# Thresholded attention and two feed-forward layers on one core: Mish as one ScalarE function, one power-of-two set per pair, other warm-up, other plan

## The chip, the core and the metric

The kernel runs on one core of one Trainium2 chip. The core's engines are TensorE (PE in the profile; PEld is its weight load), VectorE (DVE), ScalarE (ACT), GpSimd (POOL) and SyncE (SP), which only issues transfers. The metric is the device time of one execution in microseconds. Of the kernel before there are three such times, 1044.63, 1046.04 and 1046.65, median 1046.04, and one profiled execution.

## What is computed

Attention over 4 batches, 8 heads, 576 rows, 64 columns, in which a score counts only if it lies within tau of its row's maximum; then two feed-forward layers over the 2304 rows of 512, with 2048 hidden columns. The weights come as 64-bit floats.

```python
scores = scale * np.matmul(q, k.transpose(0, 1, 3, 2))
thresh = np.max(scores, axis=-1, keepdims=True) - tau
scores = np.where(scores >= thresh, scores, -1000000000.0)
attn = softmax(scores)                 # written out in the reference
x = (attn @ v), heads side by side     # 2304 x 512
h = x @ w_in;  x = (np.maximum(h, 0.0) ** 2) @ w_out          # first layer
h = x @ w2_in
sp = np.where(h > 20.0, h, np.log1p(np.exp(np.minimum(h, 20.0))))
out = (h * np.tanh(sp)) @ w2_out                              # second layer
```

## The kernel before

The kernel is written as a list of operations, and a planner in the kernel file puts them in order. Each operation (`op`) names the engines that may run it with a cost for each, the buffers that it reads (`r`), writes (`w`) or changes (`x`), and a due time. `Plan.order` builds a timetable by these costs, goes over it backwards to set the due times anew and forwards again (`fbi` times), and the program is issued in the order of the last timetable. So the table `PAR`, the numbers `BIAS` and the costs in the `op` calls set the order on every engine; each engine then runs its own queue strictly in that order and waits on semaphores.

Attention. Heads go in pairs, four pairs in each batch. A pair has four units of two heads by 128 rows and one tail unit of 64 rows of either head. `unit` issues the scores, a scan on DVE for the row maximum (`top`), the threshold (`most`: one addition), the exponential on ACT and the mask with the row sum on DVE (`mask`, both in `weigh`). A pair is of one of three kinds. "d" (direct): scores in float32, the weights of a head turned by five PE transposes (`values_direct`), values in float32 (`turned`), results turned back. "s" (split): q, k and v are scaled by powers of two (`pow2` finds them from the sums of squares, with one small PE product over the `ones` tile to add over the partitions, then four small DVE steps) and split into two float16 parts each (`split`); scores are three float16 products, the weights are split too (`high`, `low`), turned by a DMA transpose and multiplied by both parts of v. "h" (mixed): scores as in "d", values as in "s". Batch 0 is dddd, batch 1 is hhsh (`kb`), batches 2 and 3 are ssss.

Layers. Both layers work on blocks of 256 rows (nine). The numbers are held as a high and a low part, and each product is three products of parts (`passes`). Every piece of weights is converted once per layer from its 64-bit form (`weights`: `size`, `rest`, `clamp`, `shift`, `sign` or `factor` and `times`, then the high part `to_hi` and the remainder `to_lo`); layer 2's pieces take the places of layer 1's as these come free, while the last block of layer 1 still runs. `first` and `first_part` are layer 1: 24 matmuls of 256 columns into `h`, relu and square, rounding, remainder, 24 matmuls into `acc`; `x_first` brings a block of the attention's result from DRAM, turns it and makes its parts `xh` and `xo`. The nine blocks of layer 1 run between the units of attention. `second` is layer 2: two blocks at a time with 512 columns per matmul, one block alone at the end; between the two products stand exp, `cap`, log, `add`, sigmoid and `gate`, with a change of ACT's function table ahead of the exp and ahead of the sigmoid.

Start. `consts` makes `ident` and `ones` and loads tau; `warm` puts PE transposes of `ones` that nothing reads into the queue, six pairs of them at the plan's start, two and three behind the first two turnings of q and k.

Of the kernel before, what the change touches and what calls it, by code (L numbers as in the profile page):

```python
# [22 lines left out]
E20 = 485165195.40978996  # L23

# [6 lines left out]
    merge=3,  # L31
    warm=(6, 2, 3),
    won=("S", "S"),
    land=2.09,
    lag=0.886,
    turns=("h",),
    kv=(("nat0", "V1"), ("f1", "nat1"), ("KT1", "f0"), ("V0", "KT0")),
    cd=(-128.498, 12.059, -64.352),
    urg=-19.282,
    rawt=19.972,  # L40
    kinds="dddd",
    cgen=0.135,
    split=(),
    ex=dict(cw=1, cr=6, raw=13, pd=2, sc=3),
    exo=("cw", "sc", "pd", "cr", "raw"),
    blk=list((56.005, 116.765, 222.843, 298.566, 412.468, 531.531, 625.519, 840.505, 1014.576)),
    tb2=133.298,
    down2=-115.407,
    sp=(0, 3),
    off=(205.994, 56.765, 32.779, -218.536, 74.356, 29.099, -131.451, -101.025),  # L50
    ahead=(6.306, 90.66, 9.794, -93.49, 14.671, 183.136, 42.58, 390.333, 192.204, -47.067),
    start=-111.506,
    area=dict(sc=("x0", "x1"), hl=("x2",)),
    jobahead=19.363,
    fbi=7,
    stay=-17.176,
    kinds2="ssss",
    kb=("hhsh", "ssss", "ssss"),
# [23 lines left out]
class Plan:  # L82
# [6 lines left out]
    BIAS = {"V": 1.874, "A": -0.818, "P": 2.37, "S": 0.46}  # L89
# [3 lines left out]
    TICK, ENTRY = 3.4133, 1.275  # L93

# [12 lines left out]
    def op(self, opts, fn, r=(), w=(), x=(), due=0.0, load=None, tab=None, two=False, half=False):  # L107
# [93 lines left out]
    def forwards(self, succ):  # L201
# [7 lines left out]
        table, half = None, False  # L209
# [14 lines left out]
        while count < len(ops):  # L224
            best = None
            for e in engs:
# [41 lines left out]
                if e == "T" and ops[pick].half != half:  # L268
                    same = [n for _, n in now if ops[n].half == half and ops[n].due < ops[pick].due + PAR["stay"]]
                    if same:  # L270
                        pick = same[0]
# [28 lines left out]
            if e == "T":  # L300
                dur += 0.1 * (half and not o.half)
                half = o.half
# [18 lines left out]
def attention_moe_moe_kernel(ctx: ExitStack, tc: tile.TileContext, q, k, v, tau, w1i, w1o, w2i, w2o, out):  # L321
# [119 lines left out]
    K = plan.buf("const", lambda: None)  # L441

    def consts(e):
        make_identity(nc, ident)
        nc.gpsimd.memset(ones, 1.0)
# [14 lines left out]
    def weights(layer, kind, j, due, places, wplaces, merged=False):  # L460
# [17 lines left out]
        for half in range(1 if merged else 2):  # L478
# [27 lines left out]
            def upper(raw=raw):  # L506
                return raw()[:, :, 1]
# [8 lines left out]
            def size(e, w=w, upper=upper):  # L516
                if e == "A":
                    nc.scalar.activation(out=w(), in_=upper().bitcast(F32), func=AF.Abs, scale=W_SCALE)
# [41 lines left out]
            op(cost(0.09, A=0.56, P=0.71), size, r=[raw], w=[w], due=due - 4, two=2)  # L560
            op({**cost(0.11, A=0.56, P=0.71), **cost(V=0.34)}, rest, x=[raw], due=due - 3.5 + O_CV, two=2)
            op(cost(V=0.34, P=0.71), clamp, x=[w], due=due - 3 + O_CV, two=2)
            op(cost(0.06, V=0.6), shift, r=[raw], x=[w], due=due - 2 + O_CV, two=1)
# [933 lines left out]
```

## Time and profile before

| | |
|---|---|
| median of three runs | 1046.04 us |
| the profiled execution | 1046.22 us, its span 1044.4 us |
| PE busy | 1016.4 us (97%), 8582 matmuls |
| PEld busy | 885.0 us (85%) |
| ACT busy | 796.4 us (76%), 72 table loads in it: 92.4 us |
| DVE busy | 744.0 us (71%) |
| POOL busy | 51.7 us (5%) |

The page's second part cuts the span into 40 slices. By its busy digits DVE is at 9 or 8 up to about 494 us, PE at 9 from 130 us on, ACT at 7 to 9 nearly throughout. A busy share is an average over stages with different limits, and a busy PE can still be at half its clock: the granted clock of each stretch stands beside it. The first layer's first matmul comes at 131 us, the second layer's first at 641. Between the end of the last matmul and the end of the span lie the last evacuation and the last stores.

### The profile page before, as it was taken

The numbers are of one execution on the slowest core, as the hardware profiler recorded it, in microseconds if no ns is written. First come the engines' busy times: TensorE is split into PE (matmuls) and PEld (weight loads), VectorE is DVE, ScalarE is ACT, GpSimd is POOL, SyncE is SP. The second block draws the span as 40 slices with busy tenths as digits, with TensorE's granted clock in tenths as the row PEclk, the third lists the DMA queues.
The fourth block names the chain that finished last, engine by engine and source line by source line (L and its number), as shares of the span: only waits on it lengthen the run. The fifth ranks groups of instructions, "written<-read, shape, count | busy, mean of one in ns | idle before, by whom it ended". The sixth has DMA issues, their size and how long they took to land.

```text
span 1044.4 us, 22116 instructions
## 1 busy us (share of the span) xinstructions
PE 1016.4 (97%) x8582; PEld 885.0 (85%) x8582; DVE 744.0 (71%) x1693; ACT 796.4 (76%) x1277; POOL 51.7 (5%) x53
## 2 busy tenths in 40 slices
PE   6999799999999999999999999999999999999998
PEld 2666479888988898998999999978888888888897
DVE  3999999999888998998672138788754544544533
ACT  3789888886877877786794459999976877786765
POOL 0210132000010000000000000000000000000000
PEclk9999899999999999999999999999999999999999
DMA  8624467888977988887761013421100110010010
GB/s 259 176 68 146 143 141 168 154 164 150 178 156 158 164 181 159 178 170 138 189 199 66 26 66 101 142 88 53 48 34 1 41 41 1 21 41 1 1 42 20
DMA packets 238521, 111.48 MB, mean 107 GB/s; under 512 B 202320, under 2 KB 219216, under 8 KB 238416
## 3 DMA queue, kind: packets, MB, share of 16 engines
q1 hardware_dynamic: 238128, 109.55, 44.4%
q8 instruction: 67, 1.10, 0.4%
q10 hardware_dynamic: 288, 0.52, 0.1%
q14 instruction: 38, 0.31, 0.1%
HBM read 58.13 MB, written 14.16 MB: 69 GB/s over the span
## 4 chain that ended last, share of the span: by engine, by line
PE 80%; ACT 10%; DVE 5%; issue 3%; DMA 1%; SPq 0%; DVEq 0%; ACTq 0%
PE acc L428 25%; PE h L428 21%; PE s L428 20%; PE small L428 10%; ACT area L1266 2%; DVE e L900 1%; ACT L1262 1%; PE acc L750 1%; PE s L790 1%; ACT area L530 1%; PE s L1169 1%; ACT gh L576 1%; DVE area L866 1%; ACT area L554 1%; ACT e L889 1%
## 5 line engine op out<-in xcount | busy, mean ns | idle before, releaser
L428 PE MATMUL h<-xh,wi 128*128 128x256 f32 x1152 | 218.5, 282 | 0.4 <-ACT r L1214 0.4
L428 PE MATMUL acc<-gh,wo 128*128 128x256 f32 x1152 | 215.7, 280 | 0.0
L428 PEld LDWEIGHTS h<-xh,wi 128*128 128x128 f32 x1152 | 184.4, 193 | 10.3 <-issue 4.7
L428 PEld LDWEIGHTS acc<-gh,wo 128*128 128x128 f32 x1152 | 183.1, 192 | 5.5 <-issue 4.7
L428 PE MATMUL h<-xo,wi 128*128 128x256 f32 x576 | 159.0, 276 | 0.0
L428 PE MATMUL acc<-gl,wo 128*128 128x256 f32 x576 | 158.5, 275 | 0.0
L428 PEld LDWEIGHTS h<-xo,wi 128*128 128x128 f32 x576 | 111.1, 193 | 0.0
L428 PEld LDWEIGHTS acc<-gl,wo 128*128 128x128 f32 x576 | 110.6, 192 | 0.0
L428 PE MATMUL s<-KT,area 64*128 64x512 f16 (+7 forms) x820 | 95.6, 358 | 4.0 <-DVE xo L1186 2.3
L1262 ACT ACT_TABLE_LOAD x72 | 92.4, 1283 | 1.3
L587 DVE TENSOR_TENSOR gl<-r,gh 128x512 fp32r<-128x512 f32 x80 | 55.3, 691 | 51.5 <-ACT gh L576 49.8
L889 ACT ACTIVATE e<-area,m 128x576 f32<-128x576 f32 x93 | 70.6, 771 | 18.9 <-DVE area L866 8.6
L428 PE MATMUL acc<-wo,gh 128*128 128x512 f32 x240 | 79.8, 380 | 0.0
L900 DVE SCALAR_TENSOR_TENSOR e<-area,n,e 128x576 f32<-128x576 f32 x93 | 74.4, 814 | 6.0 <-ACT e L889 5.1
L576 ACT ACTIVATE gh<-r 128x512 fp32r<-128x512 f32 x90 | 56.5, 628 | 27.5 <-PE acc L428 24.3
L1214 ACT ACTIVATE r<-h 128x512 f32<-128x512 f32 x72 | 42.8, 595 | 39.8 <-PE h L428 34.4
L866 DVE TENSOR_SCALAR_CACHE_REDUCE area<-s,c 128x576 f32<-128x576 f32 x81 | 64.9, 814 | 5.3 <-PE s L428 4.5
L929 DVE TENSOR_TENSOR hl<-e,hl 128x512 f16<-128x512 f32 (+1 forms) x137 | 67.5, 499 | 1.4 <-ACT hl L924 1.1
L428 PE MATMUL small<-V,pt 128*128 128x64 f16 (+1 forms) x1680 | 65.5, 194 | 0.3 <-DMA pt<-hl 0.3
L1266 ACT ACTIVATE area<-area 128x512 f32<-128x512 f32 x108 | 63.7, 621 | 0.3
L924 ACT ACTIVATE hl<-e 128x576 f16<-128x576 f32 x77 | 52.0, 677 | 15.3 <-DVE e L900 12.0
L428 PEld LDWEIGHTS <-pt 128*128 128x128 f16 (+1 forms) x1680 | 54.9, 101 | 10.2 <-issue 7.5
(299 smaller groups left out, 2223.6 us busy)
## 6 DMA issues: line engine op xcount, KB each, us to landing
area<-in_moe_w_in_dram SPq DMA_DIRECT2D x13, 512.0 KB, 3.7
area<-in_moe_w_out_dram SPq DMA_DIRECT2D x12, 512.0 KB, 3.9
xx<-xdr SPq DMA_DIRECT2D x36, 128.0 KB, 2.6
x2dr<-stg SPq DMA_DIRECT2D x18, 256.0 KB, 2.3
xdr<-xx SPq DMA_DIRECT2D x32, 128.0 KB, 2.2
area<-in_moe_w_in_dram SPq DMA_DIRECT2D x4, 1024.0 KB, 5.5
wi<-in_moe_w_out_dram SPq DMA_DIRECT2D x3, 1024.0 KB, 5.1
f<-in_v_dram SPq DMA_DIRECT2D x12, 256.0 KB, 3.0
```

What stands on the lines that cost most here:

```text
L428: nc.tensor.matmul(o, l, r, start=start, stop=stop, skip_group_check=True)
L530: nc.scalar.activation(out=lower(), in_=lower().bitcast(U32), func=AF.Copy, scale=0.93 * 2.0 ** -29)
L576: nc.scalar.activation(out=o, in_=i, func=AF.Copy)
L587: VEC[e].tensor_tensor(out=part(lo), in0=src(), in1=f32(part(hi)), op=ALU.subtract)
L866: nc.vector.tensor_scalar(out=sc(), in0=s()[:, 0:576], scalar1=c()[:, 3:4], scalar2=None, op0=ALU.mult, op1=ALU.min, accum_out=m()[:, i:i ...
L889: lambda e: nc.scalar.activation(out=ex(), in_=sc(), func=AF.Exp, bias=m()[:, i:i + 1], scale=-1.0),
L900: nc.vector.scalar_tensor_tensor(out=ex(), in0=sc(), scalar=nt()[:, i:i + 1], in1=ex(), op0=ALU.is_le, op1=ALU.mult, accum_out=l()[:, 0, u ...
L924: nc.scalar.activation(out=hl()[:, 0:576], in_=ex(), func=AF.Copy)
L929: VEC[e].tensor_tensor(out=hl()[:, a:a + n], in0=ex()[:, z:z + n], in1=hl()[:, z:z + n], op=ALU.subtract)
L1214: nc.scalar.activation(out=halves(r()), in_=turned_out(ph()), func=AF.Relu)
L1262: nc.scalar.preload_act_table_set({"ln": "natural_log_exp_and_others", "sig": "sigmoid_and_others"}[table])
L1266: nc.scalar.activation(out=out, in_=in_, func=func, **kw)
```

## The change

It does the following.

- `second`: the six steps between layer 2's products become one ACT function, Mish, read from PSUM; its table is loaded once.
- `job`: k, q and v of a split pair share one call of `pow2` (three columns instead of two and one), so v is loaded and split in `job` too. `job_v` stays for mixed pairs.
- `warm`: single products of `ones` by `ones` into eight slices of `acc` in turn, which need only `ones`, instead of pairs of transposes into one slice; 1, 3 and 7 of them. `ones` is filled by an operation of its own, ahead of `ident`.
- The last block's sums: the two tiles of `acc` are buffers of their own, in the last step each tile's products are operations of their own, and the second tile is evacuated and stored in two halves.
- `unit`: the scores' matmuls go from 64 columns and then 512 to 512 and then 64; `most` may run on ACT.
- The plan: new numbers in `PAR`, `BIAS` and costs. By them batch 1 is dhss instead of hhsh, weights are no longer converted in double pieces (`merge` 8 instead of 3), `factor` and `times` are not used, and POOL gets nothing but constants.

```diff
-    merge=3,
-    warm=(6, 2, 3),
+    merge=8,
+    warm=(1, 3, 7),
...
-    sp=(0, 3),
+    sp=(0, 0),
...
-    kb=("hhsh", "ssss", "ssss"),
+    kb=("dhss", "ssss", "ssss"),
...
-    BIAS = {"V": 1.874, "A": -0.818, "P": 2.37, "S": 0.46}
+    BIAS = {"V": 1.26, "A": 0.34, "P": 3.463, "S": 0.46}
...
-    K = plan.buf("const", lambda: None)
+    K, K0 = plan.buf("const", lambda: None), plan.buf("ones", lambda: None)
+    op({"P": 0.5}, lambda e: nc.gpsimd.memset(ones, 1.0), w=[K0], due=-60.0)
...
+        rv = sbuf(place("f", "f0", "f1", "f2"), [128, 10, 64], F32)
...
-        isc = pow2("kq", [rk, rq], [kn, qn], due - 8)
+        isc = pow2("kqv", [rk, rq, rv], [kn, qn, V], due - 8)
...
-        job_v(p, due - O_JOB)
+        split(rv, 2, c, V, lambda: V()[:, :, 0:64], lambda: V()[:, :, 64:128], due - 5, 640)
...
+    def spin(i):
+        if not spun:
+            spun.append(psum.tile([128, 1024], F32, name="acc", tag="acc"))
+        z = 128 * (i % 8)
+        mm(spun[0][:, z:z + 128], ones, ones, True, True)
...
-                for c0, c1 in ((512, 576), (0, 512)):
+                for c0, c1 in ((0, 512), (512, 576)):
...
-        op({"V": 0.12}, most, r=[m, K], w=[nt], due=due + 1.3 - URG)
+        op({"V": 0.12, "A": 0.2}, most, r=[m, K], w=[nt], due=due + 1.3 - URG)
...
+        def mish(out, in_):
+            if not loaded:
+                nc.scalar.preload_act_table_set("mish")
+                loaded.append(1)
+            nc.scalar.activation(out=out, in_=in_, func=AF.Mish)
...
+                    op({"A": 0.48}, gate, r=[ph[z].buf], w=[gs[z]], due=d + 0.6, tab=("sig",))
+                    to_hi(gs[z], ghs[z], flat, d + 0.8)
+                    to_lo(gs[z], ghs[z], gls[z], flat, d + 0.9)
+                work = [(f, n, (0, 1)) for f in range(nf) for n in range(k)]
+                if end and st == 16 // nf - 1:
+                    work = [(f, 0, (t,)) for t in range(2) for f in range(nf)]
...
+                    for c0, c1 in ((0, 128), (128, 256)) if end and t else ((0, 256),):
```

The order on PE at the program's start, up to the second unit of scores, before (`ident,wo` are the turnings of q and k, `ident,ones` the warm-up, `KT,area` scores):

```order
L790 MATMUL s_102<-ident,wo_72 128x128 x4
L790 MATMUL s_102<-ident,wo_72 128x64
L790 MATMUL s_114<-ident,wo_72 128x128 x4
L790 MATMUL s_114<-ident,wo_72 128x64
L750 MATMUL acc<-ident,ones 128x128 x8
L428 MATMUL s_144<-KT,area 128x64
L428 MATMUL s_146<-KT,area 128x64
L428 MATMUL s_144<-KT,area 128x512
L428 MATMUL s_146<-KT,area 128x512
L750 MATMUL acc<-ident,ones 128x128 x14
L428 MATMUL s_199<-KT,area 128x64
```

And now, the same place:

```order
L435 MATMUL acc<-ones 128x128
L806 MATMUL s_114<-ident,wo_74 128x128 x4
L806 MATMUL s_114<-ident,wo_74 128x64
L806 MATMUL s_127<-ident,wo_74 128x128 x4
L806 MATMUL s_127<-ident,wo_74 128x64
L435 MATMUL acc<-ones 128x128 x4
L435 MATMUL s_150<-KT,area 128x512
L435 MATMUL s_152<-KT,area 128x512
L435 MATMUL s_150<-KT,area 128x64
L435 MATMUL s_152<-KT,area 128x64
L435 MATMUL acc<-ones 128x128 x6
L435 MATMUL s_184<-KT,area 128x512
```

Ahead of the first scores stand four products (and one at the very start) where eight transposes stood, and ahead of the second unit six where fourteen stood.

The order on DVE from its first weight conversion to the first scans of scores (`s_144`, `s_146` and `s_199` are read by the scans), before:

```order
L525 TENSOR_SCALAR stg<-stg 128x512
L542 SCALAR_TENSOR_TENSOR stg<-stg,area 128x512
L548 SCALAR_TENSOR_TENSOR stg<-area,stg 128x512
L587 TENSOR_TENSOR wi_109<-stg,wi_109 128x512
L525 TENSOR_SCALAR wo_138<-wo_138 128x512
L542 SCALAR_TENSOR_TENSOR wo_138<-wo_138,xh 128x512
L866 TENSOR_SCALAR wo_138,m_170<-s_144,cd 128x576
L866 TENSOR_SCALAR wi_188,m_170<-s_146,cd 128x576
L548 SCALAR_TENSOR_TENSOR wo_138<-xh,wo_138 128x512
L875 TENSOR_SCALAR n_207<-m_170,tt 128x2
```

And now (the scans read `s_150` and `s_152`):

```order
L555 SCALAR_TENSOR_TENSOR wo_92<-xh,wo_92 128x512
L532 TENSOR_SCALAR stg<-stg 128x512
L594 TENSOR_TENSOR wo_112<-wo_92,wo_112 128x512
L549 SCALAR_TENSOR_TENSOR stg<-stg,area 128x512
L555 SCALAR_TENSOR_TENSOR stg<-area,stg 128x512
L594 TENSOR_TENSOR wi_136<-stg,wi_136 128x512
L532 TENSOR_SCALAR stg<-stg 128x512
L549 SCALAR_TENSOR_TENSOR stg<-stg,area 128x512
L532 TENSOR_SCALAR stg<-stg 128x512
L555 SCALAR_TENSOR_TENSOR stg<-area,stg 128x512
L882 TENSOR_SCALAR wi_168,m_169<-s_150,cd 128x576
L882 TENSOR_SCALAR wo_176,m_169<-s_152,cd 128x576
```

Twelve conversion steps stand ahead of the first scan (the first two are above the piece shown) where six stood, and the threshold addition has left DVE.

The order on ACT in layer 2, one step of two blocks and the beginning of the next, before (`s_10712` is a product in PSUM, `r` and `stg` go into the rounding):

```order
L1262 ACT_TABLE_LOAD
L1266 ACTIVATE area<-s_10712 128x512 x2
L1266 ACTIVATE area<-area 128x512 x2
L1262 ACT_TABLE_LOAD
L1266 ACTIVATE area<-area 128x512 x2
L576 ACTIVATE pt_10855<-r 128x512
L576 ACTIVATE gh_10857<-stg 128x512
L1262 ACT_TABLE_LOAD
```

And now:

```order
L1282 ACTIVATE r<-s_10206 128x512
L1282 ACTIVATE stg<-s_10206 128x512
L583 ACTIVATE gh_10256<-r 128x512
L583 ACTIVATE gh_10279<-pt_10182 128x512
L1282 ACTIVATE area<-s_10266 128x512
L1282 ACTIVATE pt_10302<-s_10266 128x512
```

Two table loads and four passes of ACT have left each step.

## Rows read from the trace of the kernel before

**Rows 1.** Stretches, us: busy and instructions of each engine; PE clock, DMA share, GB/s.

```profile
0.00:26.00 26.00, 17.96 (x48) 7.67 (x48) 7.94 (x19) 10.32 (x16) 1.46 (x8) 1.00 0.90 259
26.00:104.00 78.00, 73.57 (x636) 48.90 (x637) 75.34 (x192) 65.92 (x125) 12.31 (x11) 1.00 0.43 131
104.00:130.00 26.00, 19.72 (x149) 12.98 (x151) 25.92 (x55) 21.67 (x37) 4.49 (x3) 0.90 0.50 144
130.00:156.00 26.00, 26.00 (x232) 20.46 (x230) 25.91 (x52) 23.00 (x35) 8.17 (x6) 0.90 0.63 141
676.00:702.00 26.00, 23.98 (x104) 20.40 (x104) 22.45 (x38) 25.87 (x38) 0.00 (x0) 0.93 0.18 61
754.00:780.00 26.00, 26.00 (x122) 22.79 (x121) 11.59 (x20) 18.82 (x28) 0.00 (x0) 1.00 0.11 41
```

**Rows 2.** Timeline: start, length, engine, line, operation, operands, idle before. Layer 1's beginning.

```profile
124.32 0.68 DVE L1186 TENSOR_TENSOR xo<-s,xh 128x512 fp32r<-128x512 f32 x1
...
131.53 0.58 PE L428 MATMUL h<-xh,wi 128*128 128x256 f32 x1
```

**Rows 3.** Timeline of the opening.

```profile
8.00 1.39 PE L790 MATMUL s<-ident,wo 128*128 128x128 f32 x5 [0.93 <-DMA wo<-in_q_dram]
...
15.89 7.41 PE L750 MATMUL acc<-ident,ones 128*128 128x128 f32 x14
15.99 0.82 DVE L866 TENSOR_SCALAR_CACHE_REDUCE wo<-s,cd 128x576 f32<-128x576 f32 x1 [4.02 <-PE s L428]
...
18.08 0.22 DVE L875 TENSOR_SCALAR n<-m,tt 128x2 f32<-128x2 f32 x1
18.21 0.69 DVE L542 SCALAR_TENSOR_TENSOR stg<-stg,area 128x512 int32<-128x512 int32 x1
...
18.81 0.42 DVE L525 TENSOR_SCALAR stg<-stg 128x512 f32<-128x512 f32 x1
...
23.23 2.51 PE L428 MATMUL s<-KT,area 64*128 64x64 f32 x8
...
25.77 0.82 DVE L866 TENSOR_SCALAR_CACHE_REDUCE wi<-s,cd 128x576 f32<-128x576 f32 x1 [5.94 <-PE s L428]
...
26.51 0.81 DVE L900 SCALAR_TENSOR_TENSOR e<-wo,n,e 128x576 f32<-128x576 f32 x1
```

**Rows 4.** Timeline: a subtraction on POOL and the mask on DVE beside it.

```profile
111.55 2.36 POOL L587 TENSOR_TENSOR wo<-wo,wo 128x1024 fp32r<-128x1024 f32 x1 [30.84 <-ACT wo L576]
...
112.18 2.35 DVE L900 SCALAR_TENSOR_TENSOR e<-wi,n,e 128x576 f32<-128x576 f32 x1
```

**Rows 5.** Timeline of PE: direct values, turning, direct scores; split scores, split values.

```profile
68.57 1.46 PE L428 MATMUL small<-wo,V 128*64 128x128 f32 x20
69.96 0.66 PE L972 MATMUL h<-ident,e 128*128 128x128 f32 x4
...
70.65 1.35 PE L428 MATMUL s<-KT,area 64*128 64x64 f32 x8
...
212.97 0.91 PE L428 MATMUL s<-KT,area 64*128 64x64 f16 x12
213.81 0.97 PE L428 MATMUL small<-V,pt 128*64 128x64 f16 x28
```

**Rows 6.** Groups on ACT from 624 to 754 us: count, busy us, mean ns, idle before.

```profile
L1262 ACT ACT_TABLE_LOAD x18 | 23.1, 1283 | 0.3
L1266 ACT ACTIVATE area<-area 128x512 f32<-128x512 f32 x28 | 16.5, 623 | 0.1
...
L1266 ACT ACTIVATE area<-s 128x512 f32<-128x512 f32 x14 | 8.0, 593 | 0.1
```

**Rows 7.** PE's waits after 136 us: for whom, us in total, times, longest.

```profile
PE s L428 <- DVE stg L1363: 2.4, 2, 2.0
...
PE s L428 <- DVE isckq L647: 0.3, 1, 0.3
```

**Rows 8.** Timeline of the end.

```profile
1039.59 1.08 ACT L1390 ACTIVATE area<-acc 128x512 f32<-128x512 f32 x2 [4.55 <-PE acc L428]
```

More of the change, by code (lines that the diff above doesn't have):

```diff
@@ L105, in buf, with op @@
         return b
-    def op(self, opts, fn, r=(), w=(), x=(), due=0.0, load=None, tab=None, two=False, half=False):
+    def op(self, opts, fn, r=(), w=(), x=(), due=0.0, load=None, tab=None, two=False, half=0):
         o = Op()
@@ L208, in forwards @@
         port = {"V": (0.0, 0.0), "P": (0.0, 0.0)}
-        table, half = None, False
+        table, half = None, 0
         work = {}
@@ L267, in forwards @@
                         pick = same[0]
-                if e == "T" and ops[pick].half != half:
-                    same = [n for _, n in now if ops[n].half == half and ops[n].due < ops[pick].due + PAR["stay"]]
+                if e == "T" and t > PAR["stayt"] and (ops[pick].half > 0) != (half > 0):
+                    same = [n for _, n in now if (ops[n].half > 0) == (half > 0) and ops[n].due < ops[pick].due + PAR["stay"]]
                     if same:
@@ L300, in forwards @@
             if e == "T":
-                dur += 0.1 * (half and not o.half)
+                dur += self.change(half, o.half)
                 half = o.half
@@ L852, in scores @@
                         mm(o[:, c0:c1], l, r, i == 0, i == (0 if direct else 2))
[L854 to L855 removed]
+        op({"T": (1.2 if direct else 0.85) if hh < 2 else 0.65 if direct else 0.48}, scores, r=[QT, KT], w=ss, due=due,
+           half=3 if direct else 2)
         m = sbuf(rot("m0", "m1", "m2"), [128, 2], F32)
@@ L1099, in attention @@
             p.keep = None
-            if b in PAR["split"] and PAR["kinds"][pr] == PAR["kinds2"][pr] == "d":
-                p.keep = kept.setdefault((b, pr), {})
+            p.late = b > 0 or 0 not in groups
             due = t0 + (t1 - t0) * i / n
@@ L1370, in second @@
+                for f, n, ts in work:
                     fc = nf * st + f
@@ L1411, in layer1 @@
+                        dma(store, "out" if n < 8 else "out2", r=[ot], due=d + 1, on="SA" if end else "S")
     def layer1(j):
@@ L1442, in attention_moe_moe_kernel @@
         t = blk[0] - 1 + 0.1 * j if j < 4 else due_f(0, j) - PAR["cgen"]
-        if 0 in PAR["split"] and any(int(z[2]) == j for kind in ("pd", "raw") for z in spare[kind]):
-            t = min(max(t, blk[1] - AHEAD[1] + 0.1 * j), due_f(0, j) - 0.01)
         at(t, layer1, j)
```

230 lines of the change are left out of this document (107 added, 123 removed).

## The prediction

> **What bounds the kernel now.** I read the stretches by time first, then the waits in the costliest of them, then single rows. The stretches [rows 1] show TensorE (PE) and VectorE (DVE). From 26 to 104 us DVE is busy for 75.3 of 78 us and from 104 to 130 for 25.9 of 26, while PE has 4.4 and 6.3 us of idle time there: the opening is DVE's. From 130 us PE is busy nearly without a gap; in the middle of layer 2 (754 to 780) 122 matmuls of 512 columns stand in 26 us, 213 ns each, and nothing waits. So the span is an opening that ends when layer 1 begins (the first of its matmuls stands at 131.5 us [rows 2]), then PE's own work, with one hole: in 676 to 702 PE is busy for 23.98 us at a granted clock of 0.93 [rows 1], where ScalarE (ACT) is full (25.87 of 26). A gain has to come from the opening, from that hole, from less PE work, or from the tail.
>
> **The opening.** DVE idles 18.1 us in the first 26, 2.7 up to 104 and 0.1 up to 130 [rows 1], 20.8 in all. The two large pieces are waits for PE's scores, 4.02 and 5.94 us [rows 3]. The second has a plain cause: the second unit of scores starts at 23.23, directly behind 14 warm-up transposes that take 7.41 us, 0.53 each. The order has now 4 products ahead of the first unit and 6 ahead of the second, where it had 8 and 14 transposes. At the old 0.53 for one: q is transposed at 8.00 now [rows 3]; its load moves behind a weight load on SP's queue, for which I add 1 us, so its 1.39 us end at 10.4, 4 products at 12.5, the scores (2.51) at 15.0 instead of just before 15.99, 6 products at 18.2, the second scores at 20.7 instead of just before 25.77. (SP's queue also has pair 1's k, q and v behind five more weight loads now; they are wanted only behind the third unit, and I cost that at nothing; the lower gain below covers it.) DVE meanwhile has 12 conversion steps ahead of the first scan instead of 6. It starts at about 7.2 instead of 6.2 (tau also stands one load later), works 4 x 0.42 + 8 x 0.60 = 6.5 us, waits 1.3 for the first scores, scans two (0.74 each) and does three steps (1.8), and waits 2.4 for the second. Idle: 7.2 + 1.3 + 2.4 plus the old 2.8 = 13.7. Gain 7; 10 if a product takes half of 0.53, 4 if the early loads jam.
>
> Against that stands more DVE work before layer 1's first input is ready. From the orders, up to the first subtraction that makes xo: scans and masks 38 + 36 before, 40 + 38 now, 0.74 each [rows 3]; shift and sign steps of 512 elements 24 (and 9 of double size) before, 40 now, 0.60 each (18.21 to 18.81); remainders 6 (2 double) before, 18 now; clamps 6 (4 double) before, 21 now, 0.34; 21 threshold additions (0.13, 18.08 to 18.21) before, none now. A double step goes in as two single ones less 0.09. With the small steps, nearly alike, the sums are 96.6 us before and 104.9 now, +8.3. Three of these 8.3 are two more units' scans, done early and not twice; DVE stays nearly full later, so I count half, 1.5, as saved. The 80 additions that move to ACT (at 0.2, 4 us up to there) find room: ACT is busy for 65.9 of 78 us [rows 1]; without that room they would cost those 4.
>
> What DVE loses to GpSimd (POOL) goes away, for POOL does nothing after the constants now (46 operations of before have gone to the other engines). A mask that takes 0.81 otherwise took 2.35 while POOL subtracted 1024 elements [rows 4]. DVE was busy for about 103.5 us up to the xo step at 124.32 [rows 1, 2] against the 96.6 counted; 7 is the upper bound of that loss, 0 the lower; I take 5, as most steps beside POOL in these rows are stretched. Sum of the opening: -7 - 5 + 8.3 - 1.5 = **-5.2** (bounds -12 and +4).
>
> PE's granted clock is 0.90 in 104 to 130 and in 130 to 156 [rows 1], after PE's thin time there. A tenth of the second stretch is 2.6 us of PE lost, some 1.7 of it behind 131.5. A fuller PE would keep the clock: **-1.7** (0 to -2.6).
>
> **PE's work.** Batch 1's heads go from two pairs "h" and one "s" and an "h" to d, h, s, s: in sum one direct pair and one split pair more, two mixed fewer. One direct unit of scores is 1.3 us (70.65, 1.35 long, of which the last of it overlaps with what follows), values of one direct step 1.39 (68.57 to 69.96), the five transposes of a head 0.69 (69.96 to 70.65) [rows 5]. A split unit is 0.84 plus 0.09 for entering, split values of two heads 0.9 [rows 5]. Per pair, with five units, nine turnings and five steps of values: d = 5 x 1.3 + 9 x 0.69 + 5 x 1.39 + 14 further transposes at 0.14 (q, k and the results) = 21.6; h = 5 x 1.3 + 5 x 0.9 + 10 x 0.14 = 12.4; s = 5 x 0.93 + 5 x 0.9 = 9.2. So 21.6 + 9.2 - 2 x 12.4 = **+6.0**. But by the order the added direct pair runs ahead of layer 1: one unit of scores, four heads' transposes and two steps of values, 1.3 + 2.8 + 2.8 = 6.9, are done before the first layer-1 matmul in the new order and not in the old. PE's idle time there, 10.7 us less the 5 by which the opening shrinks, holds most of it. I count 0 on the path, +6 as the bound. The merged power-of-two set drops ten tiny products of 0.1 us and their chain of four DVE steps: **-1**.
>
> **Layer 2.** Mish replaces exp, cap, log, add, sigmoid and product by one ACT operation and one table load in all. In 624 to 754 ACT loses 18 table loads (23.1 us) and the 36 log and sigmoid passes (28 of them 16.5, so 22 in all) [rows 6] of its 130; an exp from PSUM becomes a Mish from PSUM, whose time no row shows. I take that of the exp, 0.59 [rows 6], since the form is the same; less has no reason in these rows, and three times that, for the three passes it replaces, is the upper bound. DVE loses 18 each of cap, add and product, at the 0.42 and 0.69 of like steps [rows 3], 32 us. With 45 of ACT's 130 us and 32 of DVE's gone, the conversions of layer 2's weights run ahead of PE. PE's waits there were 2.4 us for DVE's product [rows 7], and the lower clock behind it cost 1.8 (0.07 of 26 us [rows 1]). In all **-4.2** (-2 to -6; a Mish of three times 0.59 would put 21 us back on ACT and leave it 24 free). From 754 on PE never waited, so 54 further table loads are off its path and bring nothing.
>
> **The tail.** After the last matmul ACT evacuates two tiles, 1.08 us [rows 8], then stores. Now the first tile's sums end six matmuls earlier, and two half tiles follow, about 0.6: **-0.6** (-0.2 to -1).
>
> Sum: -5.2 - 1.7 - 1 - 4.2 - 0.6 = -12.7. The profiled execution took 1046.22 for a span of 1044.4 and is 0.2 above the median; 1046.2 - 12.7 = **1033.5**.
>
> The score matmuls go from 64-then-512 columns to 512-then-64; the columns are the same, and I cost it at nothing.
>
> **Rivals.** *The clock rises earlier.* Here 7.41 us of transposes in a row ran at 0.53 each and the next unit of scores still took 2.51 where it later takes 1.35: at the lower level, 1.2 GHz, though the clock column, whose record starts later, reads 1.00. If products between the scores lift it to 2.4 GHz before the second unit, those scores end 1.2 sooner, the products cost 1.6 less, and DVE's second wait (2.4) vanishes: 1033.5 - 3 = 1030.5. The Trainium skill, "TensorE: Matmul & The Clock Gate", Part 4: PE-mode transpose, says that transposes do not count as PE-busy in the same way; the slow scores behind the 14 transposes agree, and by it the time would be 1030.5. No row shows products of this kind, so this rival has 0.15.
>
> *PE becomes the opening's bound.* The direct pair's 6 us find no idle time: 1033.5 + 4 to 6, say 1038. For it: PE is busy for 73.6 of 78 us in 26 to 104. Against: 6.3 idle in 104 to 130 [rows 1]. 0.20.
>
> *DVE falls behind in the middle.* POOL's work, 19 us at DVE's prices, comes back; threshold additions (80 x 0.13) and power-of-two steps (3) leave. Net +6, and without relief from the shared time that lands on a DVE that is nearly full in the opening [rows 1] and, by the page's second part, in nine tenths of every slice up to 494: 1039 to 1041. 0.13.
>
> *Slower: the joint power-of-two set holds PE.* Its product on PE now waits for k, q and v together, and PE's queue is in order, so layer 1's matmuls behind it stand. Ten pairs; it decides at 1.3 us for each pair (13 in all). At 2.0, the longest wait that PE has after 136 us [rows 7], it is +20: 1053.5. Against it: such a product shows hardly any wait in [rows 7], 0.3 once. 0.06.
>
> **How the numbers follow.** Forecast 0.46, then 0.15, 0.20, 0.13, 0.06. Its own bounds are some 6 either way. The range 1024 to 1042 leaves out the slower rival, the far part of the middle one, and less than 0.1 below. About 0.2% (2.1 us) can be told from no change. Faster 0.91: all but the slower rival and a sliver of the middle one; same 0.03; slower 0.06.
>
> **What would show it.** Right: first DVE scan near 15, second near 18 to 21; POOL empty; first layer-1 matmul at 125 to 128; one Mish table load, no PE wait over 1 us in layer 2; 213 ns per matmul at the end. Wrong: a Mish of over 1.8 us; PE waits on isckqv; PE busy below 25 of 26 between 150 and 480; layer 1 starting at 131 or later.

## The result and the profile after

The changed kernel takes 1030.38 us (median of four runs, 1029.79 to 1031.52) against 1045.91 for the kernel before (four runs, 1044.63 to 1046.65). The ratio is 0.9854, 95% interval 0.9837 to 0.9871: faster by 15.5 us (1.5%), where 12.7 were forecast. The profiled execution took 1031.52 us for a span of 1029.7, 14.7 less than the span before.

The same stretches of the kernel after, as in [rows 1] (busy time and instructions of PE, PEld, DVE, ACT, POOL, then PE's granted clock, DMA share, GB/s):

```profile
0.00:26.00 26.00, 14.68 (x60) 10.85 (x62) 14.90 (x33) 13.96 (x25) 0.84 (x7) 0.95 0.94 286
26.00:104.00 78.00, 73.63 (x664) 52.35 (x662) 76.12 (x200) 72.22 (x155) 0.00 (x0) 1.00 0.48 134
104.00:130.00 26.00, 24.75 (x232) 18.14 (x228) 24.64 (x59) 23.43 (x50) 0.00 (x0) 1.00 0.26 83
130.00:156.00 26.00, 25.44 (x219) 21.48 (x219) 25.59 (x65) 23.78 (x48) 0.00 (x0) 1.00 0.51 145
...
676.00:702.00 26.00, 26.00 (x122) 22.78 (x121) 15.08 (x24) 13.69 (x22) 0.00 (x0) 1.00 0.16 57
...
754.00:780.00 26.00, 26.00 (x122) 22.76 (x121) 3.46 (x5) 5.33 (x9) 0.00 (x0) 1.00 0.00 1
```

DVE works 14.90 us of the first 26 where it worked 7.94. POOL is empty behind the constants. The clock is at its full level from 104 us on. In 676 to 702 ACT has fallen from 25.87 to 13.69 us, and PE does 122 matmuls where it did 104. From 754 on nothing has changed for PE: 122 matmuls then, 122 now.

The timeline of the opening, to set beside [rows 2] and [rows 3]:

```profile
8.51 0.15 DVE L455 TENSOR_SCALAR tt<-tt 128x1 f32<-128x1 f32 x1 [8.51 <-DMA tt<-in_tau_dram]
...
15.24 2.40 PE L435 MATMUL s<-KT,area 64*128 64x512 f32 x8 [2.48 <-ACT area L817]
...
17.57 2.69 PE L435 MATMUL acc<-ones 128*128 128x128 f32 x12
17.67 0.82 DVE L882 TENSOR_SCALAR_CACHE_REDUCE wi<-s,cd 128x576 f32<-128x576 f32 x1 [0.27 <-PE s L435]
...
20.19 1.30 PE L435 MATMUL s<-KT,area 64*128 64x512 f32 x8
...
21.52 0.82 DVE L882 TENSOR_SCALAR_CACHE_REDUCE wo<-s,cd 128x576 f32<-128x576 f32 x1 [0.48 <-PE s L435]
...
119.27 0.69 DVE L1204 TENSOR_TENSOR xo<-s,xh 128x512 fp32r<-128x512 f32 x1
...
125.14 0.38 PE L435 MATMUL h<-xh,wi 128*128 128x256 f32 x1
```

(A float32 product stands in the trace as two matmuls, a transpose as one: the x12 above are six products.) Four points cut the span into phases that can be set side by side: the first layer-1 matmul, the first layer-2 matmul, the last matmul's start, the end.

| phase | before | after | difference |
|---|---|---|---|
| to layer 1's first matmul | 131.53 | 125.14 | -6.4 |
| from there to layer 2's first | 509.30 | 506.67 | -2.6 |
| from there to the last matmul | 398.35 | 392.38 | -6.0 |
| from there to the end | 5.24 | 5.56 | +0.3 |

One profiled execution is a sample. Ten runs below share this kernel's order on PE from layer 1 to layer 2, and their second phase lies between 504.2 and 507.6. Three of them share its opening to the letter (the doubled Mish, Abs, the tail's own tile); with the kernel after itself layer 1 starts at 123.5, 124.0, 125.1 and 125.1 in these four, the first xo at 117.6, 118.1, 119.2 and 119.3. The last two phases repeat within 0.4 and 0.1 in the runs that leave them alone.

### The profile page after: what moved, and what is told of

Same layout as the page of the kernel before. It is cut to its first block, busy times and chain, and to the rows that moved or that the text cites. A ratio compares the mean times of both kernels' runs of the same rounds, so it can differ in the third digit from the quotient of the medians.

```text
span 1029.7 us, 21534 instructions
## 1 busy us (share of the span) xinstructions
PE 1002.4 (97%) x8581; PEld 888.2 (86%) x8581; DVE 617.9 (60%) x1442; ACT 622.0 (60%) x1143; POOL 0.8 (0%) x7
## 4 chain that ended last, share of the span: by engine, by line
PE 83%; ACT 5%; DMA 5%; DVE 4%; SPq 2%; issue 1%; ACTq 0%; DVEq 0%
PE acc L435 26%; PE s L435 22%; PE h L435 21%; PE small L435 10%; DMA pt<-hl 2%; DMA area<-in_moe_w_in_dram 2%; ACT e L908 1%; SPq L792 1%; DMA f<-in_q_dram 1%; DMA area<-in_moe_w_out_dram 1%; DVE e L919 1%; PE s L1187 1%; PE h L991 0%; PE acc L991 0%; ACT stg L525 0%
## 5 line engine op out<-in xcount | busy, mean ns | idle before, releaser
L435 PE MATMUL h<-xh,wi 128*128 128x256 f32 x1152 | 213.2, 279 | 0.8 <-ACT r L1232 0.5
L594 DVE TENSOR_TENSOR gl<-r,gh 128x512 fp32r<-128x512 f32 x90 | 62.2, 691 | 157.7 <-ACT gh L583 157.4
L435 PE MATMUL s<-KT,area 64*128 64x512 f16 (+7 forms) x840 | 88.3, 333 | 3.9 <-ACT area L817 2.5
L882 DVE TENSOR_SCALAR_CACHE_REDUCE area<-s,c 128x576 f32<-128x576 f32 x90 | 71.7, 814 | 7.2 <-PE s L435 6.8
L594 DVE TENSOR_TENSOR pt<-area,pt 128x512 fp32r<-128x512 f32 x18 | 12.5, 692 | 102.1 <-ACT pt L583 102.1
L948 DVE TENSOR_TENSOR hl<-e,hl 128x512 f16<-128x512 f32 (+1 forms) x136 | 61.0, 454 | 7.3 <-ACT hl L943 7.2
L435 PE MATMUL small<-V,pt 128*128 128x64 f16 (+1 forms) x1540 | 58.9, 194 | 2.4 <-DMA pt<-hl 1.7
L435 PEld LDWEIGHTS <-pt 128*128 128x128 f16 (+1 forms) x1540 | 50.4, 101 | 10.1 <-issue 5.9
L943 ACT ACTIVATE hl<-e 128x576 f16<-128x576 f32 x68 | 46.0, 678 | 19.8 <-DVE e L919 10.3
L1282 ACT ACTIVATE r<-s 128x512 f32<-128x512 f32 x17 | 10.2, 601 | 68.4 <-PE s L435 68.4
```

The costliest lines, as they stand in the source:

```text
L435: nc.tensor.matmul(o, l, r, start=start, stop=stop, skip_group_check=True)
L594: VEC[e].tensor_tensor(out=part(lo), in0=src(), in1=f32(part(hi)), op=ALU.subtract)
L882: nc.vector.tensor_scalar(out=sc(), in0=s()[:, 0:576], scalar1=c()[:, 3:4], scalar2=None, op0=ALU.mult, op1=ALU.min, accum_out=m()[:, i:i ...
L943: nc.scalar.activation(out=hl()[:, 0:576], in_=ex(), func=AF.Copy)
L948: VEC[e].tensor_tensor(out=hl()[:, a:a + n], in0=ex()[:, z:z + n], in1=hl()[:, z:z + n], op=ALU.subtract)
L1282: nc.scalar.activation(out=out, in_=in_, func=AF.Mish)
```

## Layer 2: what Mish needs beside it

The first experiment put Mish alone into the kernel before (the edit in short).

```diff
-  exp, cap, log, add, sigmoid, product (six operations)
+  op({"A": 0.48}, gate, ...)   # mish(halves(g()), turned_out(ph[z]()))
```

> The kernel before with one part of the change alone: layer 2's six steps become one Mish from PSUM. Up to layer 2 the order is that of the kernel before; in layer 2 it is planned anew. Theory A (the forecast's term: PE's waits for DVE's product and the lower clock behind them go, 4.2 us, at most 6): from the first layer-2 product to the last matmul 392 to 394 us instead of 398.35, the start of layer 1 at 131.5 as before, time 1040 to 1041.7. Theory B (the hole in 676 to 702 comes from the weight conversions that are left over from layer 1's end, not from the activation): it stays, time 1044 to 1046.

It is slower: 1057.90 us, ratio 1.0111 (1.0093 to 1.0130). Both expectations fell. The stretches of this kernel, then ACT's groups from 640 to 735 us (count, busy us, mean ns, idle before):

```profile
676.00:702.00 26.00, 19.47 (x81) 15.82 (x81) 14.38 (x24) 24.71 (x33) 1.27 (x1) 0.87 0.43 135
702.00:728.00 26.00, 23.58 (x98) 19.23 (x97) 10.52 (x16) 15.76 (x22) 0.00 (x0) 0.93 0.07 21
```

```profile
L554 ACT ACTIVATE area<-area 128x512 f32<-128x512 f32 x8 | 6.8, 855 | 0.0
L554 ACT ACT_TABLE_LOAD x5 | 6.4, 1283 | 0.1
L1264 ACT ACT_TABLE_LOAD x5 | 6.4, 1283 | 0.1
```

L1264 is the Mish, L554 the Sign of a weight's conversion (`factor`). Each time ACT goes from one to the other it loads a table, ten times, 12.8 us, and with the first load of Mish eleven. They fall where ACT is full and PE waits for its results: PE's waits from 640 to 760 us were 2.8, and are 6.9 for ACT's `gh` and 1.9 for the remainders behind them, and the granted clock falls to 0.87 and 0.93 of full behind these waits. A further wait of 2.7 us, for ACT's `r` in layer 1, ends at 642.37, 15 us ahead of the first load of Mish at 657.75: it comes with the order planned anew and not with the tables.

The change holds two further edits that keep ACT at one table: a weight's size is taken by Copy instead of Abs, and the sign of layer 2's weights comes from DVE (`sp=(0, 0)`). Both went into the kernel before with Mish:

```diff
-    sp=(0, 3),
+    sp=(0, 0),
...
-  nc.scalar.activation(out=w(), in_=upper().bitcast(F32), func=AF.Abs, scale=W_SCALE)
+  nc.scalar.activation(out=w(), in_=upper().bitcast(F32), func=AF.Copy, scale=W_SCALE)
```

> The kernel before with Mish and with what goes with it in the change: the size of a weight by Copy instead of Abs, and the sign of layer 2's weights by DVE instead of ACT's Sign, so that one table load stands in layer 2 instead of the 12 of the run with Mish alone. The order up to layer 2 is that of the kernel before. Theory A (the 11 us lost with Mish alone are the swaps of ACT's table between Mish and the weights' Abs and Sign, at a place where ACT is full): first layer-2 product to last matmul 392 to 394 us, layer 2's start as before at 640.8 +- 1, time 1039.5 to 1041.7. Theory B (the old plan's numbers do not fit a shorter layer-2 step, whatever the tables): PE's waits for ACT's gh and the lower clock in 676 to 728 stay, time 1050 or more.

Theory A's cause, 1.1 us above its time: 1042.78 us, ratio 0.9970 (0.9958 to 0.9982), one table load behind the one at the program's start, and full stretches:

```profile
676.00:702.00 26.00, 26.00 (x122) 22.75 (x121) 20.67 (x32) 18.23 (x29) 0.00 (x0) 1.00 0.37 122
702.00:728.00 26.00, 26.00 (x122) 22.75 (x122) 3.37 (x5) 5.97 (x11) 0.00 (x0) 1.00 0.00 1
```

To compare phases whose work differs a little (here layer 2 begins at 644.5 us, where 640.8 was expected, with 24 matmuls of layer 1 fewer left), I added up, from layer 2's first matmul on, by how much the distance between two starts of matmuls exceeds what the same kind takes undisturbed: 5.7 us before, 13.6 with Mish alone, 1.4 with all three edits, 0 in the kernel after. So Mish with its two edits is worth 4.4 us in the old plan, and the new plan takes the rest. Of the 11.2 us by which the profiled execution with Mish alone was longer, 7.9 are these; 4.4 lie ahead of layer 2's first matmul, the wait for `r` and the lower clock behind it, and the opening was 1.1 shorter. The two edits together also take Sign off ACT, 24 passes of 20 us in all, so this run does not separate that from the loads; the next one does. The time fell by 2.9 us (interval 1.9 to 4.4).

The opposite edit tests the one word in the kernel after:

```diff
-  ... func=AF.Copy, scale=W_SCALE)
+  ... func=AF.Abs, scale=W_SCALE)
```

> The kernel after with one word changed, Copy back to Abs in the weights' first step on ACT; the order of the instructions is unchanged but for 9 ACT table loads between layer 2's first Mish and its last weight conversion, at 1.28 us each 11.5 us. Theory A (ACT is full there, so the loads push the conversions that PE waits for): PE waits in 640 to 700 and loses clock behind it, the time is 4 to 12 us longer, 1034 to 1042. Theory B (ACT has slack in layer 2, as the doubled Mish showed): 1030.4 +- 1.

The loads come, four and four (eight, not the nine written ahead):

```profile
L525 ACT ACT_TABLE_LOAD x4 | 5.1, 1283 | 0.1
L1282 ACT ACT_TABLE_LOAD x4 | 5.1, 1283 | 0.1
```

PE loses 2.3 us of layer 2 where it lost none, by loads alone; the time is 1031.82 (0.9874, 0.9857 to 0.9891), 1.4 above the kernel after, which the intervals do not separate. It lies between the two theories: 10 us more ACT work, of which the shorter layer-2 step absorbs most. The Trainium skill, "ScalarE: Activation LUTs", Table sets: the hidden batching unit, says that cheap functions such as abs stand in every table set. Here they do not: a program with Abs and Mish carries the loads above, and with Copy in Abs's place one, that of Mish itself, behind the one at the start.

How much room ACT has by now was asked with every Mish issued twice:

```diff
-            nc.scalar.activation(out=out, in_=in_, func=AF.Mish)
+            for _ in range(2):
+                nc.scalar.activation(out=out, in_=in_, func=AF.Mish)
```

> The kernel after with every Mish issued twice into the same tile, 72 more ACT passes of 0.59 us, 42 us of ACT work; nothing else moves. Theory A (layer 2 has room: ACT is busy for 13.7 us of the 26 in 676 to 702 and for 5.3 in 754 to 780): nothing on PE's path, first layer-2 product to last matmul stays at 392.4 +- 0.5, time 1030.4 +- 0.8; the price of a Mish, unknown when the forecast was made, did not matter up to twice its size. Theory B (the chain product, Mish, rounding, remainder is what PE waits for): 0.6 us for each of 36 steps or for the first few of a group, 1032 or more, up to 1050.

Theory A by the time: 1029.86 us (0.9846, 0.9830 to 0.9861), no longer than without. Layer 2 is 393.6 us long instead of 392.4, a little beyond the half us that theory A allowed, so 42 us more of ACT work cost 1.3. The unknown price of Mish, which the forecast bounded at three times 0.59, is 0.59 to 0.60, and it did not matter.

## The opening: DVE

For DVE up to the first subtraction that makes xo, I took for each form of instruction the lower quartile of its durations, each counted up to the next one's start where they overlap, as its undisturbed price; what its instructions took beyond that is called stretch.

| DVE up to the first xo, us | before | after | forecast for after |
|---|---|---|---|
| idle | 20.8 | 13.7 | 13.7 |
| work at undisturbed prices | 96.2 | 104.3 | 104.9 |
| stretch | 7.3 | 1.2 | 5 less |
| first xo at | 124.3 | 119.3 | 5.2 less, with 1.5 saved |

The stretch is taken to be POOL's doing. To see POOL's price alone, it got work back (the edit in short):

```diff
     def to_lo(src, hi, lo, part, due, k=1):
         def fn(e):
+            moved[0] += 1
+            if moved[0] <= 24 and moved[0] % 2:
+                e = "P"
```

> The kernel after with every second one of the first 24 remainder subtractions (128x512) on POOL instead of DVE; the order is unchanged. They all lie in the opening, and 12 of them at 0.69 us take 8.3 us off DVE. Theory A (POOL costs DVE what the kernel before shows, 6.1 us more stretching for some 16 us of POOL work, 0.38 for each): 12 at 1.2 us or a little more cost DVE 5 to 6 us, it gains 2 to 3, the first xo at 116.5 to 117.5 instead of 119.3, layer 1 at 122 to 123, time 1027.5 to 1028.5. Theory B (what POOL takes it takes from DVE in full): xo at 119.3 +- 0.7, time as the kernel after. Theory C (POOL's subtractions are late themselves and DVE or ACT waits for them): xo later than 120.

```profile
30.52 1.70 POOL L599 TENSOR_TENSOR wi<-stg,wi 128x512 fp32r<-128x512 f32 x1 [10.51 <-ACT wi L583]
30.97 1.53 DVE L532 TENSOR_SCALAR stg<-stg 128x512 f32<-128x512 f32 x1
...
39.95 1.68 POOL L599 TENSOR_TENSOR wo<-stg,wo 128x512 fp32r<-128x512 f32 x1 [7.74 <-ACT wo L583]
40.41 1.76 DVE L599 TENSOR_TENSOR wi<-wo,wi 128x512 fp32r<-128x512 f32 x1
```

The clamp of 0.42 us takes 1.53 beside POOL, the subtraction of 0.69 takes 1.76. Nine of the twelve lie ahead of the first xo: DVE's work falls by 5.4 us, its stretch grows by 5.3, and its idle time by 2.1, since results from POOL come later. The first xo stands at 121.3, layer 1 at 127.1, the time is 1032.06 (0.9865, 0.9850 to 0.9880), 1.7 above the kernel after, though the intervals overlap. Theory B for the exchange, with some of C: the nine ran on POOL for 13.4 us, so DVE lost 0.40 us for each us of POOL. A subtraction frees DVE of 0.60 us, runs for 1.48 on POOL, and takes 0.59 back. So the 6.1 us of stretch that are gone with POOL paid for most of the 8.1 us of added work.

The first wait, for tau until 8.51 us, was the largest left:

```diff
+    def fill(e):
+        nc.scalar.dma_start(out=tt[:, 3:4], in_=tau.to_broadcast([128, 1]))
+        nc.gpsimd.memset(ones, 1.0)
...
-        nc.sync.dma_start(out=tt[:, 3:4], in_=tau.to_broadcast([128, 1]))
```

> The kernel after with tau's load issued on ACT's queue as the first thing of the program instead of fifth on SP's; nothing else moves. In the kernel after DVE's first instruction waits for tau until 8.51 us, while its first weight conversion has had its inputs since 5.6. Theory A (DVE sets the end of the opening, so an idle us taken from it comes back whole): DVE starts at 5.5 to 6, ACT's evacuations of k and q, which stand behind ACT steps that wait for DVE, come about 2.5 us earlier and with them the first scores (15.24 now), layer 1 starts at 122 to 123.5 instead of 125.1, time 1027.5 to 1029. Theory B (another wait is last: loads of the weights or of k and q): the time taken from the first wait turns up in the next ones, layer 1 at 124.5 to 125.1, time 1029.8 to 1030.4.

```profile
5.32 0.15 DVE L457 TENSOR_SCALAR tt<-tt 128x1 f32<-128x1 f32 x1 [5.32 <-DMA tt<-in_tau_dram]
...
9.30 0.43 DVE L534 TENSOR_SCALAR stg<-stg 128x512 f32<-128x512 f32 x1 [1.57 <-ACT stg L527]
...
13.65 2.40 PE L435 MATMUL s<-KT,area 64*128 64x512 f32 x8 [0.58 <-ACT area L819]
...
18.71 1.30 PE L435 MATMUL s<-KT,area 64*128 64x512 f32 x8
...
123.53 0.38 PE L435 MATMUL h<-xh,wi 128*128 128x256 f32 x1
```

DVE starts 3.2 us earlier; half of it comes back as a wait for the next weights (the 1.57 in the second row). The first scores come 1.6 earlier, as ACT's evacuation of q stood behind steps that wait for DVE. Layer 1 starts at 123.5, the early end of the 123.5 to 125.1 that the unchanged opening shows, so the profile alone does not show the gain. The times do, 1028.17 us (0.9830, 0.9815 to 0.9845): its slowest, 1028.67, lies below the fastest of the kernel after, 1029.79, though the two intervals still overlap by a little. The truth lies between A and B, nearer to A.

## The opening: PE's warm-up and the added pair

Three runs change the warm-up alone. Transposes in place of the ten later products, into eight slices:

```diff
-        mm(spun[0][:, z:z + 128], ones, ones, True, True)
+        nc.tensor.transpose(spun[0][:, z:z + 128], ones, ident)   # all but the very first
```

> The kernel after with the ten warm-up products that follow the first turnings replaced one for one by PE transposes of the same tile; the order on every engine is unchanged. Theory A (the forecast's: a product and a transpose cost the same 0.53 us and the clock is not theirs): the second unit of scores stays at about 1.3 us, the second pair of scans starts at 21.5 as in the kernel after, layer 1 starts at 125.1 +- 0.5, time 1030.4 +- 0.7. Theory B (the products lift the clock, transposes do not): the second unit of scores takes 2.4 to 2.5 us, its scan starts at 22.7 to 23.5, layer 1 starts 1 to 2 us later, time 1031.5 to 1033.

The same into one slice, as before the change (`z = 896`):

> The kernel after with the ten later warm-up products replaced by transposes as in the other run, but all into one slice of the accumulator, as in the kernel before, instead of eight in turn. Theory A (a transpose into the slice of the one ahead of it waits for that one): 0.53 each as in the kernel before instead of 0.25, the second unit of scores starts at 20.5 to 21.5 and takes 2.4, the granted clock's rise moves from 20 us to 23 or later, layer 1 0.5 to 2 us later. Theory B (the slice does not matter; the 0.53 of the kernel before was the lower clock): 0.25 to 0.27 each, clock at 20 us, times as with transposes into eight slices.

And no products at all (`lambda e: None`):

> The kernel after without any warm-up product; the order of everything else is unchanged. Theory A (the products hold the second scores up and give nothing back): the second unit starts at 17.6 instead of 20.2 and, at the lower clock, ends at 20.1 instead of 21.5, its scan starts 1.3 us earlier, layer 1 starts up to 1.3 earlier, time 1029 to 1030. Theory B (the products pay by the clock): scores and turnings up to 30 us or later run at the lower level, 2.4 to 2.5 us for a unit, DVE waits for the third and fourth unit too, layer 1 starts 1 to 3 us later, time 1031.5 to 1033.5.

PE's timeline with transposes into eight slices, into one, and without any:

```profile
17.68 1.54 PE L765 MATMUL acc<-ident,ones 128*128 128x128 f32 x6
19.15 1.81 PE L435 MATMUL s<-KT,area 64*128 64x512 f32 x8
```

```profile
16.88 1.55 PE L765 MATMUL acc<-ident,ones 128*128 128x128 f32 x6
18.35 2.23 PE L435 MATMUL s<-KT,area 64*128 64x512 f32 x8
```

```profile
18.27 3.12 PE L435 MATMUL s<-KT,area 64*128 64x512 f32 x8 [0.91 <-DVE wi L882]
...
25.07 2.40 PE L435 MATMUL s<-KT,area 64*128 64x512 f32 x8
```

In the trace's record the granted clock first reaches its full level (2.4 GHz) at 32.8 us in the kernel before, 19.9 in the kernel after, 20.0 with transposes into eight slices, 20.0 into one, 28.8 without warm-up. So products bring the clock up no earlier than transposes, and the slice does not matter. The second scores took 1.30 us behind products, and 1.81 and 2.23 behind transposes: six transposes are over in 1.5 us where six products take 2.7, so more of these scores lies ahead of 20.0 us. A transpose here starts 0.21 to 0.27 us behind the one ahead; in the kernel before it was 0.53 [rows 3]. The trace of before shows why: twenty of its 22 transposes wait for the one ahead, 7.0 us in all, on a semaphore that it sets. Each of them asked for a new `acc` tile, and the change takes one tile for all (`spun`); no run put the new tiles back, but at the same lower clock the spacing is 0.21 without them. PE stood still for a good half of the warm-up that should have kept it busy.

Times: 1029.76 with transposes into eight slices (0.9853, 0.9835 to 0.9870), 1028.93 into one (0.9839, 0.9826 to 0.9853), 1030.57 with nothing (0.9856, 0.9835 to 0.9878); layer 1 at 124.8, 123.9 and 125.5. These intervals overlap each other and that of the kernel after. The clock comes up 9 us later without warm-up, and costs some tenths: DVE waits 0.37 us for the second scores there and 1.06 for the third, 0.48 and 0.50 with the products. In what was expected, the lower clock of those scores was right (3.12 and 2.40 us), its price of 1 to 3 us was not. In the four executions with one opening the record falls back at about 23.4 us, behind a wait of PE for DVE's mask, in the two in which layer 1 starts at 125.1, and not there in the two at 123.5 and 124.0. That the one brings the other is not shown: with transposes into one slice it falls back too, and layer 1 starts at 123.9.

Then PE got more work of the kind that the direct pair adds (the edit in short):

```diff
-            for i in range(5):
+            for _ in range(2 if turned_n[0] <= 30 and turned_n[0] % 3 == 0 else 1):
+                for i in range(5):
```

> The kernel after with every third of the first 30 turnings of weights done twice, ten times five PE transposes, some 6.6 us of PE work ahead of layer 1's start; the order is unchanged and no other engine has more to do. Theory A (the forecast's: up to layer 1 PE has idle time, and the added direct pair of about this size cost nothing): layer 1 starts at 125.1 to 126, time 1030.4 to 1031.3. Theory B (PE sets the end of the opening as much as DVE does): layer 1 starts at 128 to 131, time 1033 to 1036.

Its stretch of 26 to 104:

```profile
26.00:104.00 78.00, 75.58 (x681) 55.53 (x679) 73.98 (x194) 69.68 (x148) 0.00 (x0) 1.00 0.50 136
```

PE finds 1.9 of the 6.6 us in its idle time there, and DVE loses 2.1 us of work, now waiting for PE. Layer 1 starts at 127.05. That is between the theories: about 2 to 3 of 6.6 us land on the path. The time is 1033.15 (0.9874, 0.9852 to 0.9896), with runs from 1030.7 to 1034.9, so this size is rough. In the profiled executions of this run and of the one with POOL, layer 2 starts at 631.9 and 631.6, as in the kernel after (631.8), although layer 1 starts 2 us later; whether layer 1 gives such a delay back is open, as the medians say it does not.

## The end

The kernel after loses 0.3 us behind the last matmul. Its timeline, where [rows 8] stood:

```profile
1024.60 1.15 ACT L1389 ACTIVATE area<-acc 128x512 f32<-128x512 f32 x3 [4.55 <-PE acc L435]
```

All three evacuations stand behind the last matmul, the first tile's too. Both tiles are halves of one PSUM tile, and the program's waits know only the whole. The second half got a tile of its own:

```diff
-  parts = [plan.buf(f"acc{t}", lambda t=t, z=z: z()[:, 512 * t:512 * t + 512]) for t in range(2)]
+  parts = [plan.buf("acc0", lambda z=z: z()[:, 0:512]), pbuf("h", [128, 512])]
...
-  z = rot("s0", "s1", ("h", "o0")) if single else rot("s0", "s1")
+  z = rot("s0", "s1", ("h", "o0")) if single and not end else rot("s0", "s1")
```

> The kernel after with the last block's second tile of sums in a PSUM tile of its own (the one that the last block's first products then no longer use in turn); the order of the last block shifts a little, nothing before it. In the kernel after the first tile's evacuation starts only behind the very last matmul, 0.42 us after that matmul's start, although its own sums end 2.6 us earlier. Theory A (both halves of one PSUM tile are released together): now the first evacuation starts some 2.5 us before the last matmul ends, two half evacuations of 0.65 us stand behind it instead of three of 1.15, time 0.5 to 0.9 shorter, 1029.5 to 1029.9. Theory B (the end hangs on the stores' landing alone, 2.5 to 2.9 us): 0 to 0.2 shorter.

From the last matmul's start to the end 4.90 us instead of 5.56, with only the two halves behind the last matmul (which starts at 1022.79):

```profile
1023.21 0.66 ACT L1388 ACTIVATE area<-h 128x256 f32<-128x256 f32 x2
```

Theory A's cause, not its distance: the plan takes the two tiles' products in turn, three matmuls each, so with names of their own the first tile's sums are seen to end three matmuls, 0.65 us, ahead of the end, not the 2.6 that was expected. Those 0.65 are the gain in the trace; the time, 1029.66 us (0.9847, 0.9833 to 0.9862), is 0.7 lower, which its interval does not separate from the kernel after.

## A faster version

Tau first on ACT's queue, and the separate tile at the end:

> The kernel after with tau's load first on ACT's queue and the last second tile in a PSUM tile of its own. Theory A (the two gains are at both ends of the program and add: 1.5 to 2.2 and 0.6): 1027.3 to 1028.3, layer 1 at 122.5 to 123.7, last matmul's start to end of span 4.9 us. Theory B (the earlier start of layer 1 is given back in layer 1, whose pace DVE and the attention set): 1029 to 1030.

Theory A: 1027.47 us, ratio 0.9825 (0.9811 to 0.9838), some 3 us faster than the kernel after, whose interval just touches it. Layer 1 starts at 123.4, the end takes 4.91 us.

## The prediction, step by step

- **What bounds the kernel.** Right: the opening, one hole in layer 2, PE's own work between. The three places gave 6.4, 6.0 and 2.6 us.
- **DVE's idle time.** The sum is exact (13.7 forecast, 13.7 measured), its parts are not, so that it is exact is luck; the other three executions of this opening show 12.2 to 13.7. DVE was put at 7.2 us and began at 8.51 with tau; the first scan was put at 15 and came at 17.67. The step that failed took PE to be ready for the scores as soon as its products were done; PE waited 2.48 us for ACT's evacuation of q, which stood behind conversions. Against that the second scan comes 3.9 us behind the first, where 5.7 were forecast, since the second scores ran at the higher clock (1.30 us for 2.51) and the six products ahead of them took 2.7 us for 3.2.
- **DVE's work** +8.3: measured +8.1. **POOL** -5: stretch -6.1. Both terms hold, and the run with POOL put back shows that POOL's work stretches DVE's; that all of the 6.1 was POOL's is inferred from it. The half of 3 us that was counted as saved cannot be seen: -7.1, +8.1 and -6.1 make the 5.05 by which xo moved. Layer 1's first matmul moved by 6.4, and its second input by 6.3 (128.36 to 122.05). But what stands between them is another thing now. Before, PE waited for that step and then did one unit of scores at the lower clock:

```profile
129.09 2.50 PE L428 MATMUL s<-KT,area 64*128 64x64 f32 x8 [2.26 <-DVE xo L1186]
```

In the kernel after PE waits for nothing from 118.96 us on: 1.24 us of turnings and the same scores, 1.30 us at the full clock, keep it until 125.14. The opening ends with PE's queue, and DVE is no longer alone in setting it.

- **A product at the old 0.53.** The figure nearly holds (2.08 us for the first four, 2.69 for the next six), the reason does not: the old 0.53 was 0.21 of work and a wait for the transpose ahead.
- **PE's clock behind 104 us.** Right: 1.00 in both stretches. The record of before is at the lower level from 128.4 to 135.2, and of the 3.7 us behind 131.5 half, 1.8, is lost.
- **PE's work.** 6 for the added kinds with 6.9 ahead of layer 1 and 1 for the pair's powers was counted as 0 and -1; by its own figures -1.9 is left behind layer 1's start. That is too little. From layer 1's to layer 2's start PE's time without its waits and the clock's loss falls from 505.9 to 501.4 us, by 4.5 (501 to 502 in all ten runs); one cause is the small powers product, nine fewer of two matmuls of 0.11 us each, so -2 and not -1. With the clock's 1.8 this makes -6.3, and PE's waits there grow from 1.6 to 5.2 us, which the forecast did not have: phase two shows -2.6, and -1.7 to -5.1 over the ten runs. That the 6.9 cost nothing ahead of layer 1 was too kind: of 6.6 us added by an experiment 2 to 3 arrived.
- **Layer 2**, -4.2, bounds -2 to -6: measured -6.0, at the bound; 4.4 of it by Mish with its tables. The mechanism was right (waits and the clock behind them), the size too small, as the hole's whole 5.7 us went. The step left out is the one that mattered most: the forecast took the table loads as gone with Mish. They go only with Abs and Sign gone, two edits that it did not cost; without them layer 2 lost 7.9 us in the old plan instead of gaining. A Mish at the exp's 0.59 was right.
- **The tail**, -0.6: failed, +0.3. The step that failed is "the first tile's sums end six matmuls earlier": where the two tiles can be told apart it is three, and in the kernel after the first evacuation waits for the last matmul all the same, so nothing was taken away: the third evacuation ends 0.1 later, and what stands behind it, three stores instead of two, takes 0.2 more.
- **Order of the scores**: 0, and nothing speaks against it. No run tests it alone, nor batch 1 as dhss, the joint power-of-two set or the threshold on ACT.
- **Rivals.** *The clock rises earlier*: it did, at 19.9 us, and the second scores took 1.30. It gave 1030.5, which is the time measured, but by luck, for the 3 us it priced were not there: without any warm-up the time is the same, because the second scores then start 1.9 us earlier and end no later, and DVE waits 0.4 us for them either way. The Trainium skill, "TensorE: Matmul & The Clock Gate", Part 4: PE-mode transpose, says that transposes do not count as PE-busy in the same way. No run supports it: the clock rose at 20.0 us with six transposes as with six products and at 28.8 with neither, though the transposes stood between two units of scores and not alone. The waits between the old transposes are the nearer reason for the late clock of the kernel before. *PE becomes the bound*: in part. *DVE falls behind in the middle*: no, in the 130 us from 260 on DVE is busy for 113.64 where it was for 118.42. *The joint power-of-two set*: no wait for it among PE's waits behind layer 1's start, which are led by

```profile
PE small L435 <- DMA pt<-hl: 1.7, 2, 1.3
PE s L1187 <- ACT xh L1199: 1.4, 2, 0.7
PE h L435 <- ACT r L1232: 0.5, 1, 0.5
```

By phases of the profiled executions the forecast was -5.2, -2.7 (powers and clock), -4.2 and -0.6; measured were -6.4, -2.6, -6.0 and +0.3. The 2 us more that were gained there are 1.8 of layer 2 and 1.2 of the opening, less 0.9 at the end.

## What to carry to other kernels

A new activation function is worth what its table lets the other functions on ACT do: look for every function that runs near it and change those that would swap the table, or the gain turns into a loss. Where DVE is full, work put on POOL beside it can cost DVE as much as it saves; measure the exchange by the stretch of DVE's own instructions. Filler work keeps an engine busy only if nothing makes it wait for itself (and was worth at most some tenths here), and a result can leave early only if it does not share its tile with sums still running.

## What was not expected of the hardware

- With Mish's table in place, Abs and Sign each brought a table load, and Mish another on the way back, 1283 ns each; Copy and Relu brought none.
- DVE lost 0.40 us for each us of a two-input float32 subtraction on POOL (5.3 of 13.4), and a clamp that took 0.42 took 1.53 beside it.
- The granted clock's first rise differed between runs of one opening by up to 7 us (12.6 with the doubled Mish, falling back until 19.4; 19.7 to 20.1 in three others), with no more than 1.7 us in the start of layer 1.
